# A new instruction order for the first third of a scan-and-FFN kernel, with four small edits

## The chip, the core and the metric

The kernel runs on one core of a Trainium2 chip. A core has five engines with a queue each, which the texts call by short names: PE (TensorE, matrix products; PEld is its loading of the stationary operand), DVE (VectorE), ACT (ScalarE), POOL (GpSimd) and SP (SyncE, which here only issues transfers). Each engine takes its own instructions strictly in the order in which the program gave them, and waits on semaphores for the others. Transfers (DMAs) issued by SP and ACT run on sixteen DMA engines beside all of this. Operands lie in SBUF; products are written to PSUM, which has eight banks of 128 x 512 float32 here.

The metric is the device time of one execution in microseconds (us).

## The reference

One sequence of 2048 tokens with 512 features in bfloat16 goes through a layer norm; the normed tokens go two ways, through a diagonal complex recurrence and through a gated feed-forward net, and the two are multiplied and added to the input:

```python
xn = _layernorm(x)                                   # 2048 x 512
# A: recurrence with 512 complex states
dt = exp(log_dt); Lam_bar = exp(dt * Lam)            # Lam = Lambda_re + i Lambda_im
Bu = xn @ (((Lam_bar - 1) / Lam)[:, None] * Bmat).T
h[t] = Lam_bar * h[t - 1] + Bu[t]                    # over all 2048 tokens
s = 2 * real(h @ Cmat.T) + xn * Dskip
# B: gated FFN, 1376 hidden features
f = (gelu(xn @ w_gate) * (xn @ w_up)) @ w_down
out = x + s * silu(f)
```

## The kernel before

**Tiling.** The tokens are cut into four slabs of 512, and each slab into four tiles of 128 tokens (M = 4). A slab is normed into `xna` (tokens on partitions), turned by one transposing DMA into `xnT` (features on partitions, `dma_t4`), and then used three times:

- `half(s, h)`: the input of the recurrence, two halves of the states a slab. A half is four groups of four products (L528, stationary `BT`, moving `xnT`), each group filling a PSUM bank, which ACT copies to `U` (L530). DVE then turns `U` by the angle tables `tab` into `W` (L540, L548, L552), runs four scans (L559) and turns back into `hst`. That makes the complex recurrence a real one.
- `gate_tile(s, m)`: up and gate products of a tile (L433), evacuated by ACT as copy and gelu (L436) into `ub` and `gt`, multiplied on DVE into `at`; `at_t` transposes `at` by DMA into `atT`; `down_pair` multiplies with the down weights `wd` (L465, eleven products a tile), and ACT evacuates silu into `g2`.
- `skip(s, m)`: `xn * Dskip` on DVE.

`y_tile` then has ACT seed a bank with the skip, PE add `hst @ C2` (L481, eight products), and DVE multiply with `g2` and add x (L486, L491) into an output buffer `ot`, which SP stores. The very last tile is done in two halves of 256 columns (`HD`).

**Slab 0** goes another way, since nothing may wait at the start. Its tiles are only centered (`center`), transposed on PE (`head_t`) and multiplied with the up weights at once (`up_rows`, L382, row block by row block as weights land, and `first_w`, L401); the scale 1/std is applied when ACT evacuates (`out_up`, L391). The up weights come in four row blocks, so that products start with the first. `scale0` makes the normed tokens for `dma_t4(0)` later.

**Tile 0 of slab 0** is on everybody's way. Its mean is made by two engines at once, ACT from the last 128 columns and DVE from the first 384 (L338, L340), then one DVE instruction subtracts both parts (L342) and PE transposes it in two pairs (L312). Before that, PE runs seven products on constants (`dummies`, L295), and between tile 0's and tile 1's transposes one more (`fill`, L301). `parameters` transposes the recurrence's raw parameters `pv` (L584, L585), from which DVE and POOL make the decay `rho`, the step `dt` and the angles.

**The order.** All of this is written as 672 numbered steps. A step is a closure that emits one or a few instructions of one engine (or one DMA), with the steps that it depends on. The functions only record steps; a fixed tuple, found beforehand, says in which order they are emitted, and so each engine's and each DMA queue's order:

```python
for i in ORDER:
    emit, deps = self.steps[i]
    assert deps <= done
    emit()
```

PSUM is shared out as six `ring` banks in turn (`bank()`) and two `ybank`; a group of products can start when the ACT or DVE step that read its bank last is done. A DMA of SP or ACT uses one of eight semaphores in turn, so it is also held until the DMA eight before it has landed.

The lines that the change touches are `ORDER` (L21), `dummies` (L292), `fill` (L298), `center` (L333), `y_part` (L472), and the place where `fill` is called (L644).

Of the kernel before, what the change touches and what calls it, by code (L numbers as in the profile page):

```python
# [11 lines left out]
ALU = mybir.AluOpType  # L12
# [6 lines left out]


ORDER = (  # L21
# [23 lines left out]
)  # L45


# [33 lines left out]
def kernel(  # L81
# [17 lines left out]
    nc = tc.nc  # L99
    P = 128  # L100
# [8 lines left out]
    NS = S // TS  # L109
# [51 lines left out]
    tF = sb("tF", [P, 2, D], FP32)  # L161
    junks = [sb(f"junk{i}", [P, D]) for i in range(2)]
    junk_n = [0]

    def junk():
        junk_n[0] += 1
# [17 lines left out]
    def pe(n, cols, emit, reads=(), writes=(), **kw):  # L184
        return pl.add(PE, n * (cols + 6) / 2400.0, emit, reads, writes, lag=0.22, **kw)
# [106 lines left out]
    def dummies(k, i):  # L292
        def f():
            for j in range(k):
                T.matmul(ybank[j][:] if j < 2 else ring[i][:], lhsT=warm[:, 0:P], rhs=warm, start=True, stop=True)  # L295
        pl.add(PE, k * 0.427, f, [], [("bank", i), ("y", 0), ("y", 1)], lag=0.22, not_before=0.6)

    def fill(k, i):  # L298
        def f():
            for _ in range(k):  # L300
                T.matmul(ring[i][:], lhsT=warm[:, 0:P], rhs=warm, start=True, stop=True)  # L301
        pe(k, 512, f, [], [("bank", i)])

    def head_t(m):

# [27 lines left out]
    def center(m):  # L333

        x = x_tok[:, m, :]
        if m == 0:
            c = 3 * P
            acts(D - c, lambda: act(out=junk()[:, 0 : D - c], in_=x[:, c:D], func=AF.Copy, scale=1.0 / D, accum_out=mb[:, 0:1]),  # L338
                 [("x", 0, 0)], ["mb"], ptr=1, rank=400.0)
            dve(c, lambda: V.tensor_scalar(out=yg[0][:, 0:c], in0=x[:, 0:c], scalar1=1.0 / D, scalar2=None, op0=ALU.mult, op1=ALU.add,  # L340
                                           accum_out=ma[:, 0:1]), [("x", 0, 0)], [("yg", 0, 0), ("ma", 0)], base=0.15, rank=400.0, after=early)
            head.append(dve(512, lambda: V.tensor_scalar(out=xn[0], in0=x, scalar1=ma[:, 0:1], scalar2=mb[:, 0:1], op0=ALU.subtract, op1=ALU.subtract),  # L342
                            [("x", 0, 0), ("ma", 0), "mb"], [("xc", 0, 0), ("xc", 0, 1)], rate=2.3, rank=400.0, after=head[-1:]))
            return
        nmean, key = ma[:, m : m + 1], ("ma", m)
        sums0.append(acts(512, lambda: act(out=junk()[:], in_=x, func=AF.Copy, scale=-1.0 / D, accum_out=nmean), [("x", 0, m)], [key], ptr=2, rank=400.0 - 20 * m))
        dve(512, lambda: V.tensor_scalar(out=xn[m], in0=x, scalar1=nmean, scalar2=None, op0=ALU.add),
            [("x", 0, m), key], [("xc", m, 0), ("xc", m, 1)], rate=2.3, rank=330.0 - 20 * m)
# [123 lines left out]
    def y_part(s, m, c0, c1, bank, key, seed, e):  # L472

        w = c1 - c0
        ps = bank[:, 0:w]
        if seed:
            acts(w, lambda: act(out=ps, in_=sk[s % 2][:, m, c0:c1], func=AF.Copy), [("sk", s % 2, m)], [key])  # L477

        def f():
            for j in range(2 * NPT):  # L480
                T.matmul(ps, lhsT=hst[s % 2][:, j // NPT, j % NPT, m * P : (m + 1) * P], rhs=C2[:, j // NPT, j % NPT, c0:c1],  # L481
                         start=(j == 0 and not seed), stop=(j == 2 * NPT - 1), skip_group_check=True)
        pe(2 * NPT, w, f, [("hst", s % 2, 0), ("hst", s % 2, 1)] + C2S + ([key] if seed else []), [key])
        gi, b = g2s[s, m]
        if seed:
            dve(w, lambda: V.tensor_tensor(out=yg[e][:, c0:c1], in0=ps, in1=g2[gi][:, b, c0:c1], op=ALU.mult), [key, ("g2", gi, b)], [("yg", e, c0)])  # L486
        else:
            ys = tF[:, 0, c0:c1]
            dve(w, lambda: V.tensor_tensor(out=ys, in0=ps, in1=sk[s % 2][:, m, c0:c1], op=ALU.add), [key, ("sk", s % 2, m)], [("tF",)])
            dve(w, lambda: V.tensor_tensor(out=yg[e][:, c0:c1], in0=ys, in1=g2[gi][:, b, c0:c1], op=ALU.mult), [("tF",), ("g2", gi, b)], [("yg", e, c0)])  # L490
        dve(w, lambda: V.tensor_tensor(out=ot[e][:, c0:c1], in0=yg[e][:, c0:c1], in1=x_tok[:, s * M + m, c0:c1], op=ALU.add),  # L491
            [("yg", e, c0), ("x", s, m)], [("ot", e, c0)], rate=2.0)
        mg = s * TS + m * P
        dma(SP, 0.35, 1.5, lambda: nc.sync.dma_start(out=out_td[mg : mg + P, c0:c1], in_=ot[e][:, c0:c1]), [("ot", e, c0)], [("out", s, m, c0)], svc=(2, 0.4, 0.9))

    def y_tile(s, m):
        i = y_n[0] % 2
# [143 lines left out]
    rstd(0, 1)  # L641
    for m in range(1, M):
        norms = rstd(m, m + 1)
    fill(1, 0)  # L644
    head_t(1)
    up_rows(0, 0)
    up_rows(1, 0)
# [174 lines left out]
```

## Time and profile before

| what | us |
|---|---|
| median of three runs (179.24 to 179.58) | 179.26 |
| the profiled execution, known by its span | 178.6 |
| PE busy | 173.4 |
| DVE busy | 156.4 |
| ACT busy | 125.2 |
| POOL busy | 12.0 |

The span goes from the first to the last instruction of the profiled execution; what lies around it is not in the profile. In rows of a timeline the first number is the start in us from the span's start, the second how long the row lasted (several alike in a row are merged, with their number after the x), and in brackets stands the idle time before it and who ended it. `PE`, `DVE`, `ACT` and `POOL` are work, a `q` behind the name is the engine's sequencer, which for `SPq` is the issue of a DMA, not the transfer. In groups, busy time and the mean of one instruction (ns) follow the bar. A product of 512 columns shows 379 ns in such a group, but products overlap: what counts is the distance of their starts.

By stretches of the span, PE, DVE and ACT were busy so:

| stretch, us | PE | DVE | ACT |
|---|---|---|---|
| 0 to 10 | 9.08 | 5.43 | 5.88 |
| 10 to 20 | 10.00 | 6.96 | 9.65 |
| 20 to 30 | 10.00 | 10.00 | 9.60 |
| 30 to 40 | 9.18 | 9.69 | 8.73 |
| 40 to 50 | 10.00 | 7.78 | 8.68 |
| 50 to 60 | 10.00 | 9.51 | 9.41 |
| 60 to 70 | 10.00 | 8.35 | 9.63 |

### The profile page before, as it was taken

To read this page: it belongs to the slowest core of one execution; us is meant where nothing else is said; L and a number is where in the kernel's file an instruction comes from. 1 tells how busy PE (TensorE), PEld (TensorE's weight loads), DVE (VectorE), ACT (ScalarE), POOL (GpSimd) and SP (SyncE) were. 2 spreads that over 40 slices of the span, in tenths; PEclk is the share of its full clock that TensorE was granted. 3 is DMA by queue.
4 is the path that set the end of the run, shared out by engine and by line. 5 is a ranking of instruction groups with operands and counts; after the bars stand their busy time and mean duration, and the time that the engine had idled before them with its cause. 6 is when DMAs were issued, how large, how long until landed. Compare 5 with 4: busy or idle time off the path is not lost.

```text
span 178.6 us, 2428 instructions
## 1 busy us (share of the span) xinstructions
PE 173.4 (97%) x850; PEld 82.8 (46%) x850; DVE 156.4 (88%) x252; ACT 125.2 (70%) x240; POOL 12.0 (7%) x25
## 2 busy tenths in 40 slices
PE   7999999899999999999999999999999999999992
PEld 2555544344445544444445454444444455444451
DVE  3729999999599995899979999899999999999663
ACT  6679999797998999889578865373148618582340
POOL 2462040000200000000040000000000000000000
PEclk9999999999999999999999999999999999999999
DMA  5999999999000809814000075094000006536111
GB/s 159 338 372 188 176 227 315 150 211 228 2 0 0 196 2 173 110 59 81 0 0 6 6 124 129 25 195 84 0 0 0 0 29 155 69 58 135 53 64 60
DMA packets 47507, 18.66 MB, mean 104 GB/s; under 512 B 40232, under 2 KB 46472, under 8 KB 47496
## 3 DMA queue, kind: packets, MB, share of 16 engines
q1 hardware_dynamic: 47472, 18.52, 48.6%
q8 instruction: 6, 0.10, 0.3%
q14 instruction: 5, 0.04, 0.1%
q10 hardware_dynamic: 24, 0.00, 0.0%
HBM read 6.46 MB, written 2.10 MB: 48 GB/s over the span
## 4 chain that ended last, share of the span: by engine, by line
PE 81%; DVE 7%; DMA 6%; ACT 2%; POOL 0%; issue 0%; DVEq 0%
PE ring L433 31%; PE ring L465 20%; PE ybank L481 15%; PE ring L528 12%; DMA atT<-at 5%; PE ring L382 3%; ACT at L391 2%; DVE st L278 1%; DVE Q L620 1%; DMA x_tok<-in_A_x_dram 1%; DVE at L415 1%; DVE yg L486 1%; DVE tab L620 1%; DVE ot L491 1%; DVE sk L364 1%; ACT junk L351 0%
## 5 line engine op out<-in xcount | busy, mean ns | idle before, releaser
L433 PEld LDWEIGHTS <-xnT 128*128 128x128 bf16 x288 | 28.2, 98 | 28.4
L465 PE MATMUL ring<-wd,atT 128*128 128x512 bf16 (+1 forms) x176 | 39.5, 379 | 0.8 <-DMA atT<-at 0.7
L433 PE MATMUL ring<-wg,xnT 128*128 128x512 bf16 (+1 forms) x144 | 31.6, 357 | 0.0
L433 PE MATMUL ring<-wu,xnT 128*128 128x512 bf16 (+1 forms) x144 | 31.3, 357 | 0.0
L528 PE MATMUL ring<-xnT,BT 128*128 128x512 bf16 x128 | 30.1, 379 | 0.0
L559 DVE TENSOR_TENSOR_SCAN Fs<-rho,ini,W 128x512 bf16<-128x512 f32 x24 | 29.7, 1270 | 0.1
L436 ACT ACTIVATE ub<-ring 128x512 bf16<-128x512 f32 (+1 forms) x36 | 19.2, 555 | 14.1 <-PE ring L433 14.0
L481 PE MATMUL ybank<-C,hst 128*128 128x512 bf16 x120 | 27.7, 379 | 0.0
L465 PEld LDWEIGHTS <-atT 128*128 128x128 bf16 (+1 forms) x176 | 17.1, 98 | 22.1 <-DMA atT<-at 1.2
L530 ACT ACTIVATE U<-ring 128x512 bf16<-128x512 f32 x32 | 18.3, 601 | 8.0 <-PE ring L528 8.0
L436 ACT ACTIVATE gt<-ring 128x512 bf16<-128x512 f32 (+1 forms) x36 | 19.5, 555 | 3.7 <-PE ring L433 3.5
L481 PEld LDWEIGHTS <-hst 128*128 128x128 bf16 x136 | 13.3, 98 | 14.0
L528 PEld LDWEIGHTS <-BT 128*128 128x128 bf16 x128 | 12.5, 98 | 14.7
L540 DVE TENSOR_TENSOR Q<-U,tab 128x4096 bf16<-128x4096 bf16 x8 | 18.3, 2291 | 1.0 <-ACT tab L627 0.7
L468 ACT ACTIVATE g<-ring 128x512 f32<-128x512 f32 x16 | 9.3, 595 | 13.6 <-PE ring L465 13.5
L540 DVE TENSOR_TENSOR Q<-Fs,tab 128x4096 bf16<-128x4096 bf16 x8 | 18.3, 2287 | 0.1
L486 DVE TENSOR_TENSOR yg<-ybank,g 128x512 bf16<-128x512 f32 x15 | 10.2, 685 | 5.7 <-PE ybank L481 5.6
L740 ACT ACTIVATE junk<-x_tok 128x512 bf16<-128x512 bf16 x16 | 10.0, 636 | 1.2 <-DMA x_tok<-in_A_x_dram 1.2
L477 ACT ACTIVATE ybank<-sk 128x512 f32<-128x512 bf16 x15 | 9.0, 601 | 1.7 <-DVE yg L486 1.6
L745 ACT ACTIVATE xna<-x_tok,nb,rs 128x512 bf16<-128x512 bf16 x12 | 9.6, 817 | 0.0
L401 PE MATMUL ring<-wg,W 128*128 128x512 bf16 (+1 forms) x48 | 9.5, 357 | 0.0
L559 DVE TENSOR_TENSOR_SCAN Fs<-rho,W 128x512 bf16<-128x512 f32 x8 | 9.3, 1210 | 0.1
(126 smaller groups left out, 171.7 us busy)
## 6 DMA issues: line engine op xcount, KB each, us to landing
out_dram<-ot SPq DMA_DIRECT2D x15, 128.0 KB, 1.7
x_tok<-in_A_x_dram SPq DMA_DIRECT2D x3, 512.0 KB, 9.0
wg<-in_B_w_gate_dram SPq DMA_DIRECT2D x1, 1376.0 KB, 8.1
wd<-in_B_w_down_dram SPq DMA_DIRECT2D x1, 1280.0 KB, 8.7
wu<-in_B_w_up_dram SPq DMA_DIRECT2D x4, 256.0 KB, 3.6
x_tok<-in_A_x_dram SPq DMA_DIRECT2D x4, 128.0 KB, 2.3
wu<-in_B_w_up_dram SPq DMA_DIRECT2D x1, 352.0 KB
atT<-at SPq DMA_TRANSPOSE x16, 3.8
```

The source lines that it names most:

```text
L401: T.matmul(ps[:, 0 : b - a], lhsT=xcT[:, k, m * P : (m + 1) * P], rhs=wt[:, k, a:b], start=(k == 0), stop=(k == KT - 1))
L433: T.matmul(ps[:, 0 : b - a], lhsT=xnT[:, s % 2, m, k, :], rhs=wt[:, k, a:b], start=(k == 0), stop=(k == KT - 1))
L436: acts(b - a, lambda: act(out=dst[:, a:b], in_=ps[:, 0 : b - a], func=AF.Copy if up else AF.Gelu_apprx_tanh), [("bank", r)], [key], table= ...
L465: T.matmul(ps[:], lhsT=atT[:fs, k, m * P : (m + 1) * P], rhs=wd[:fs, k, :], start=(k == 0), stop=(k == NFT - 1))
L481: T.matmul(ps, lhsT=hst[s % 2][:, j // NPT, j % NPT, m * P : (m + 1) * P], rhs=C2[:, j // NPT, j % NPT, c0:c1], start=(j == 0 and not seed ...
L486: dve(w, lambda: V.tensor_tensor(out=yg[e][:, c0:c1], in0=ps, in1=g2[gi][:, b, c0:c1], op=ALU.mult), [key, ("g2", gi, b)], [("yg", e, c0)])
L528: T.matmul(ps[:], lhsT=BT[:, ri, k, pt * P : (pt + 1) * P], rhs=xnT[:, s % 2, :, k, :], start=(k == 0), stop=(k == KT - 1))
L530: acts(512, lambda q=q, ri=ri, ps=ps: act(out=U[ui][:, ri, q, :], in_=ps[:], func=AF.Copy), [("bank", r)], [("U", ui, q, ri)])
L540: dve(4096, lambda: V.tensor_tensor(out=Qf, in0=src.unsqueeze(1).to_broadcast(WQ), in1=table, op=ALU.mult), reads, ["Q"], rate=2.0)
L559: pl.add(DVE, 1.12 if s == 0 else 1.185, lambda ri=ri, q=q, pt=pt, first=first: V.tensor_tensor_scan(out=Fs[:, ri, q, :], data0=rho[:, pt ...
L740: acts(512, lambda i=i, fn=fn, sc=sc, m=m: act(out=junk()[:], in_=x_tok[:, s * M + m, :], func=fn, scale=sc, accum_out=sx[:, s, i, m : m + ...
L745: acts(512, lambda m=m: act(out=xn[m], in_=x_tok[:, s * M + m, :], func=AF.Identity, scale=rs[:, s, m : m + 1], bias=nb[:, s, m : m + 1]), ...
```

## The change

1. `ORDER` is written anew. PE's and ACT's sequences differ up to the gate products of slab 1 and DVE's up to the first y tiles; behind that they are the same. Of SP, the transfers change as below; of POOL, the identity now comes first, the iotas stand behind `dt`, and `ch` and `sh` have moved.
2. `fill` and its call are gone; `dummies` ends with a product of 256 columns more.
3. `center(0)`: ACT's part of the mean is 192 columns instead of 128, DVE's 320 instead of 384. The subtraction is two instructions of 256 columns. In the new order the second half (columns 256 to 511) is emitted first.
4. The last tile's output goes to a third buffer, `junks[0]`, instead of `ot[1]`.

ACT's order at the start was: table load and Silu on a constant (`tiny`), three parameter loads, the means. Now it is: the three parameter loads, a table load, the means of tiles 0 to 2, one eviction, the squares of tile 1, a second table load and Silu, and then the squares of tile 2, the mean of tile 3 and the first Sin.

SP's order, from the gate weights on (the ones before are alike):

| before | after |
|---|---|
| gate weights | gate weights |
| down weights, last 96 rows | slab 1's tokens |
| slab 1's tokens | BT, real part (transposing) |
| Drow | Drow |
| BT, real part (transposing) | xnT of slab 0 |
| xnT of slab 0 | BT, imaginary part |
| BT, imaginary part | down weights, last 96 rows |
| atT of tile 0 | down weights, the other 1280 rows |
| down weights, the other 1280 rows | atT of tile 0 |
| slab 2's tokens | atT of tile 2 |
| atT of tile 2 | atT of tile 1 |
| atT of tile 1 | slab 2's tokens |
| xnT of slab 1 | xnT of slab 1 |
| atT of tile 3 | atT of tile 3 |
| C, real and imaginary | C, real and imaginary |
| slab 1: atT of tile 0 | xnT of slab 2 |
| slab 3's tokens | slab 3's tokens |
| xnT of slab 2 | slab 1: atT of tile 2 |
| slab 1: atT of tile 2, of tile 1 | slab 1: atT of tile 0, of tile 1 |

On ACT, the squares and sums of slab 2's tokens (L740) stand among the evictions of `U` of slab 0's second half in both orders: before, three of them stand ahead of its last three evictions; after, the first stands behind the first silu of slab 0's down products and ahead of one eviction of `U`. On DVE, the coefficients of C (L685 to L703) move from among the `scale0` steps to behind the gate product (`at`) of slab 0's tile 1, and the first two products of the angle tables (L620) move ahead of the last `scale0`.

```diff
 ORDER = (
-    19, 24, 17, 18, 16, 14, 15, 13, 25, 0, 20, 12, 21, 1, 22, 2, 23, 3, 4, 27, 26, 5, 39, 6, 28, 7, 29, 41, ...
+    21, 23, 22, 12, 0, 26, 25, 34, 1, 40, 2, 42, 3, 4, 5, 27, 6, 15, 29, 28, 30, 31, 33, 46, 20, 47, 44, ...
...
     junk_n = [0]
+    ot.append(junks[0])
...
         def f():
             for j in range(k):
                 T.matmul(ybank[j][:] if j < 2 else ring[i][:], lhsT=warm[:, 0:P], rhs=warm, start=True, stop=True)
-        pl.add(PE, k * 0.427, f, [], [("bank", i), ("y", 0), ("y", 1)], lag=0.22, not_before=0.6)
-
-    def fill(k, i):
-        def f():
-            for _ in range(k):
-                T.matmul(ring[i][:], lhsT=warm[:, 0:P], rhs=warm, start=True, stop=True)
-        pe(k, 512, f, [], [("bank", i)])
+            T.matmul(ring[i][:, 0:HD], lhsT=warm[:, 0:P], rhs=warm[:, 0:HD], start=True, stop=True)
+        pl.add(PE, (k + 0.5) * 0.427, f, [], [("bank", i), ("y", 0), ("y", 1)], lag=0.22, not_before=0.6)
...
         if m == 0:
-            c = 3 * P
+            c = 320
...
-            head.append(dve(512, lambda: V.tensor_scalar(out=xn[0], in0=x, scalar1=ma[:, 0:1], scalar2=mb[:, 0:1], op0=ALU.subtract, op1=ALU.subtract),
-                            [("x", 0, 0), ("ma", 0), "mb"], [("xc", 0, 0), ("xc", 0, 1)], rate=2.3, rank=400.0, after=head[-1:]))
+            for i in range(2):
+                h = slice(i * HD, (i + 1) * HD)
+                dve(HD, lambda h=h: V.tensor_scalar(out=xn[0][:, h], in0=x[:, h], scalar1=ma[:, 0:1], scalar2=mb[:, 0:1], op0=ALU.subtract, op1=ALU.subtract),
+                    [("x", 0, 0), ("ma", 0), "mb"], [("xc", 0, i)], rate=2.3)
             return
...
-        dve(w, lambda: V.tensor_tensor(out=ot[e][:, c0:c1], in0=yg[e][:, c0:c1], in1=x_tok[:, s * M + m, c0:c1], op=ALU.add),
-            [("yg", e, c0), ("x", s, m)], [("ot", e, c0)], rate=2.0)
+        o = 2 if (s, m) == (NS - 1, M - 1) else m % 2
+        dve(w, lambda: V.tensor_tensor(out=ot[o][:, c0:c1], in0=yg[e][:, c0:c1], in1=x_tok[:, s * M + m, c0:c1], op=ALU.add),
+            [("yg", e, c0), ("x", s, m)], [("ot", o, c0)], rate=2.0)
...
-        dma(SP, ... out=out_td[mg : mg + P, c0:c1], in_=ot[e][:, c0:c1]) ...
+        dma(SP, ... out=out_td[mg : mg + P, c0:c1], in_=ot[o][:, c0:c1]) ...
...
-    fill(1, 0)
     head_t(1)
```

More of the change, by code (lines that the diff above doesn't have):

```diff
@@ L490, in y_part @@
             dve(w, lambda: V.tensor_tensor(out=yg[e][:, c0:c1], in0=ys, in1=g2[gi][:, b, c0:c1], op=ALU.mult), [("tF",), ("g2", gi, b)], [("yg", e, c0)])
-        dve(w, lambda: V.tensor_tensor(out=ot[e][:, c0:c1], in0=yg[e][:, c0:c1], in1=x_tok[:, s * M + m, c0:c1], op=ALU.add),
-            [("yg", e, c0), ("x", s, m)], [("ot", e, c0)], rate=2.0)
+        o = 2 if (s, m) == (NS - 1, M - 1) else m % 2
+        dve(w, lambda: V.tensor_tensor(out=ot[o][:, c0:c1], in0=yg[e][:, c0:c1], in1=x_tok[:, s * M + m, c0:c1], op=ALU.add),
+            [("yg", e, c0), ("x", s, m)], [("ot", o, c0)], rate=2.0)
         mg = s * TS + m * P
-        dma(SP, 0.35, 1.5, lambda: nc.sync.dma_start(out=out_td[mg : mg + P, c0:c1], in_=ot[e][:, c0:c1]), [("ot", e, c0)], [("out", s, m, c0)], svc=(2, 0.4, 0.9))
+        dma(SP, 0.35, 1.5, lambda: nc.sync.dma_start(out=out_td[mg : mg + P, c0:c1], in_=ot[o][:, c0:c1]), [("ot", o, c0)], [("out", s, m, c0)], svc=(2, 0.4, 0.9))
     def y_tile(s, m):
```

46 rows, old and new, of the table ORDER are left out of this document.

## The prediction

> **What bounds the kernel now.** I read the page's busy line first, then the chain that ended last, then TensorE's own timeline from 0 to 75 us, because the edits end there.
>
> ```profile
> PE 173.4 (97%) x850; PEld 82.8 (46%) x850; DVE 156.4 (88%) x252; ACT 125.2 (70%) x240; POOL 12.0 (7%) x25
> ...
> PE 81%; DVE 7%; DMA 6%; ACT 2%; POOL 0%; issue 0%; DVEq 0%
> ```
> TensorE is the bound: a change pays only where it removes TensorE work or a TensorE wait. Its timeline (start, duration) shows where those are:
>
> ```profile
> 4.06 0.61 PE L312 MATMUL ring<-ident,xna 128*128 128x128 bf16 x4 [0.16 <-DVE xna L342]
> 4.74 0.61 PE L301 MATMUL ring<-const-bfloat16-1.0 128*128 128x512 bf16 x1
> 5.14 0.63 PE L327 MATMUL ybank<-ident,xna 128*128 128x128 bf16 x4
> 5.57 0.75 PE L382 MATMUL ring<-wu,W 128*128 128x512 bf16 x2
> 6.16 0.39 PE L327 MATMUL ybank<-ident,xna 128*128 128x128 bf16 x4
> ...
> 24.76 7.07 PE L528 MATMUL ring<-xnT,BT 128*128 128x512 bf16 x32
> 31.96 2.54 PE L465 MATMUL ring<-wd,atT 128*128 128x512 bf16 x11
> 35.19 4.93 PE L465 MATMUL ring<-wd,atT 128*128 128x512 bf16 x22 [0.69 <-DMA atT<-at]
> 39.95 2.75 PE L528 MATMUL ring<-xnT,BT 128*128 128x512 bf16 x12
> ```
> From 35.19 to 39.95 are 22 products: 0.216 us each. So L528's 32 end at 24.76 + 6.92 = 31.68 and the next starts 0.28 later; its 11 end at 34.34 and the next starts 0.85 later. These **1.13 us** are the only waits I find between 6 and 75 us. The first is the down weights (issued 23.19, 8.7 to landing: 31.9), the second atT of tile 2. The queue shows why:
>
> ```profile
> 21.48 1.66 SPq L449 DMA_TRANSPOSE atT<-at  x1
> 23.19 0.70 SPq L664 DMA_DIRECT2D wd<-in_B_w_down_dram  x1
> 23.93 0.69 SPq L216 DMA_DIRECT2D x_tok<-in_A_x_dram  x1
> 25.86 8.45 SPq L449 DMA_TRANSPOSE atT<-at  x2
> 34.41 2.21 SPq L359 DMA_TRANSPOSE xnT<-xna  x1
> ```
> Two transposes stood behind 1.8 MB of copies. At the head:
>
> ```profile
> 0.72 1.28 ACT L252 ACT_TABLE_LOAD   x1 [0.72 <-PEq L806]
> 2.90 0.31 ACT L338 ACTIVATE junk<-x_tok 128x128 bf16<-128x128 bf16 x1 [0.69 <-DMA x_tok<-in_A_x_dram]
> 3.59 0.41 DVE L342 TENSOR_SCALAR xna<-x_tok,ma,mb 128x512 bf16<-128x512 bf16 x1
> 4.32 0.35 DVE L347 TENSOR_SCALAR xna<-x_tok,ma 128x512 bf16<-128x512 bf16 x1 [0.31 <-ACT junk L346]
> ```
> Until about 5.9 TensorE runs at half rate: four transposes take 0.63 at 5.14 and 0.39 at 6.16.
>
> **The change, part by part.** The new order puts ACT's three parameter loads first, then a table load of its own for the first Copy, and a second one at Silu: ten loads instead of nine. The loads' issues ended at 1.97 before; now the table load runs 1.9 to 3.2, and x (landed 2.88) waits for it. With 64 columns more (0.63 for 512 and 0.31 for 128: 0.05) ACT's part is out at 3.65 instead of 3.31; DVE's, 64 columns shorter, at 3.39. Subtraction starts at 3.68 instead of 3.59. A half costs 0.28 (L491's 256 columns take 0.29, its 512 0.42; 0.41 x 0.29/0.42); two overlap by 0.05 and end at 4.19 instead of 4.00. The new order makes the second half first, while TensorE's first transposes need the first half, so halving hides nothing: transposes start at 4.24 instead of 4.06. The half product more in the warm-up (0.21, to 3.96) and tile 0's parameter transposes (their inputs landed by 3.55) fit before that: free.
>
> Tile 1's transposes wait for L347 (still 4.36 to 4.71, set by ACT's mean of tile 1, landed 3.54), run 4.75 to 5.18, and the first L382 starts at 5.18 instead of 5.57: the filler (0.43) is gone, some of it spent on the later center. That is 0.39 at half rate, **-0.2** once the rate is full. Bounds: -0.4 (all at full rate) and +0.1 (the center 0.3 later still).
>
> [...]
>
> To 24.76 the lead must survive. ACT's second load and Silu (1.48, about 6.1 to 7.6) stand before the squares of tile 2, the mean of tile 3 and Sin; ACT idled 1.62 there (until 8.20). Tile 3's mean is then out at 8.9, its subtraction at 9.5, its transposes due at 10.1. The first eviction starts near 10.4 (10.31 before), first bank reuse is due 0.5 after it. On DVE the seventeen coefficient instructions (13.75 to 15.45) move behind slab 0's tables (first read by tF, 46.98), two table products (1.2 each) move ahead of tile 3's scaling, and DVE's idle 1.77 at 13.75 is filled: xna is complete at 15.3 instead of 16.2. So L528 starts at 24.56. The memsets put among DVE's work (0.06 to 0.07 each) are covered by DVE's wait for tile 0's gelu near 19; iota (0.6, now behind dt on POOL) by the 0.7 that DVE needs for the copy and statistics before it can use it. Without that cover Sin slips by 0.6.
>
> SP: the weights' tail (0.70) and Drow (0.67) no longer precede BT's first transpose, which was issued 7.55 to 15.62: it ends about 0.6 earlier, Drow follows (first read, by skip, near 21), xnT is issued at 15.7 instead of 16.25, BT's second half lands at 23.3 (23.8), due at 25.4. The down weights no longer wait for atT(0) (1.66), so they are issued at 21.6 and, at 8.7, land at 30.3, due 31.5: **-0.28**. atT(0) is now behind them, ready only at 23.9, since DVE does its gate product after statistics and tables. Bounds: it lands at 30.8 (copies done 29.5, one transpose 1.2 as between atT(2), 35.14, and atT(1), 36.31) or 32.4 (1.9 behind the copies, as atT(2) behind slab 2: 33.3 and 35.14). I take 31.7, the latter shortened for the missing slab: wait **+0.2**. atT(2) and atT(1) follow at 32.9 and 34.1, due 34.1 and 36.4: **-0.85**.
>
> Slab 2 (512 KB) moves behind atT(1), issued near 32. Bounds: 3.9 to landing as slab 3 had alone (59.24, 63.1), 9.4 as before: 35.9 to 41.4. With 1.4 MB less ahead of it, it is near the first: 36.5. It now has someone behind it: ACT's first square of slab 2 stands before an eviction of U whose bank slab 1's first L528 needs at about 38.8. Square and eviction take 0.62 + 0.53, so from landing 37.5 on TensorE waits one for one. xnT of slab 1 follows slab 2: 2.5 long (36.3 to 38.83 before), so 38.8 to 39.2 against 38.85; bounds 0 and 0.7, I take **+0.2**.
>
> From 40 to 65, ACT's tF comes earlier (DVE lost 1.95 waiting for it at 48.19), and y of slab 0 one product earlier (L481 at 66.37 before, its hst done 65.8). ACT is 94% busy from 50 to 60; bounds 0 and 0.4 of bank waits, **+0.1**.
>
> The last tile's own buffer: 0. Its L491 rows at 175.05 and 175.71 waited for no store: that of slab 3's tile 1, made by 172.89, had landed (1.7 by the DMA list) at 174.6. The cover is 0.4; a store slower by more would turn the edit into a gain.
>
> Sum: -0.2 - 0.28 - 0.85 + 0.2 + 0.2 + 0.1 = **-0.83**. The profiled execution is known by its span, 178.6; 177.8 then. The runs' median, 179.26, lies 0.66 over the span, so 178.4.
>
> **The rivals.**
> 1. The transposes stay late. Upper ends of atT(0) and xnT plus 0.4: 179.26 - 0.2 - 1.13 + 0.9 + 0.7 + 0.4 = 179.9; with half of these waits 178.9. For: transposes issued behind copies sat in the queue, BT's first for 8.07, the two atT for 8.45. Against: 0.5 MB less stands ahead of them.
> 2. Slower: slab 2's tokens stall ACT, ACT holds U's bank, TensorE waits. From landing 38.5 the whole gain is gone (0.83, and the 0.2 of xnT that the same wait covers); at 39.5 the time is 178.4 + 2.0 - 0.2 = 180.2. For: 9.4 before. Against: less ahead of it.
> 3. TensorE's full rate comes later. Rows bound it: half rate lasted 5.1 us (0.76 to 5.9); if it lasted as long again after the first L382 (5.18), the 4.4 us from 5.9 to 10.3 would be worth half: +2.2, 180.6. [...]
> 4. The new table switch costs more than its row, say two loads (2.56): ACT's mean starts at 4.46, the first L382 near 6.3, all at full rate, 0.6 behind before: 178.4 + 0.8 = 179.2. Against: no ACTIVATE in the trace waits after a load.
>
> [...]
>
> **How the numbers follow.** Forecast 0.50 (own range 177.7 to 178.9), rivals 0.24, 0.15, 0.08, 0.03. 0.2% is 0.36 us, about what runs (179.24 to 179.58) can tell from no change. Faster means under 178.9, slower over 179.6. Rival 1 gives 0.02 faster, 0.16 same, 0.06 slower; rival 2 0.02 same, 0.13 slower; rival 3 slower; rival 4 same: 0.52, 0.21, 0.27. The range, 177.7 to 180.2, leaves out the upper part of rivals 2 and 3 (0.15) and little below.
>
> **What would show it.** Two table loads before 8 us; L312's like at 4.24; first L382 at 5.18; no gap before the second and third down product, a small one before the first; slab 2 landed before 37.5; L528 of slab 1 at 39.0. Wrong if TensorE idles beside ACT's square of slab 2, or if half rate lasts past 6.5.

## The result and the profile after

The changed kernel takes 180.18 us (median of 16 runs, 178.98 to 182.66) against 179.30 (16 runs, 178.60 to 179.99): 1.0058 times the time before, 95% interval 1.0035 to 1.0082. (The ratio leaves out the longest run, of 182.66; the two medians by themselves give 1.0049.) It is slower by 0.6%; I had forecast 178.4.

Yet its profiled execution has a span of 177.4, 1.2 *shorter* than the one of before, and looks as the prediction wanted it. Its page, busy line (16 of its 850 product records are missing) and chain that ended last:

```profile
PE 171.9 (97%) x834; PEld 82.5 (47%) x850; DVE 155.8 (88%) x253; ACT 126.3 (71%) x241; POOL 13.5 (8%) x25
...
PE 94%; DMA 2%; DVE 1%; SPq 1%; issue 1%; DVEq 0%
```

TensorE's timeline of the same execution (start, duration):

```profile
4.39 0.40 PE L308 MATMUL ring<-ident,xna 128*128 128x128 bf16 x4 [0.22 <-DVE xna L340]
4.85 0.40 PE L323 MATMUL ybank<-ident,xna 128*128 128x128 bf16 x4
5.32 0.59 PE L380 MATMUL ring<-wu,W 128*128 128x512 bf16 x2
...
24.60 7.07 PE L527 MATMUL ring<-xnT,BT 128*128 128x512 bf16 x32
31.50 7.30 PE L463 MATMUL ring<-wd,atT 128*128 128x512 bf16 x32
38.64 5.34 PE L527 MATMUL ring<-xnT,BT 128*128 128x512 bf16 x24
```

From 24.60 to 38.64 are 65 products at 0.216 (32 and 33, of which the row shows 32, since one record is missing): neither wait of before is left. The marks of the prediction, for this execution: transposes 4.39 (4.24 forecast), first up product 5.32 (5.18), first half 24.60 (24.56), down weights landed 28.96 (30.3), atT of tile 0 30.98 (31.7), slab 2 35.88 (36.5), slab 1's first half 38.64 (39.0), span 177.4 (177.8).

So two profiles say faster and the runs say slower. The reason is which executions were profiled. Of every run of the experiments, and of the changed kernel's 16, both the time and the span are known, and the time was 1.73 to 1.86 over the span in every one, for every kernel here. The profile of before, 178.6, is thus an execution of about 180.4, longer than all 16 of its runs. Of 148 executions of the kernel before that were measured beside the experiments below, the median span is 177.5, and six reach 178.6. Of 28 executions of the changed kernel (16 and the 12 of e1) the median span is 178.8, and two are at 177.4 or less. I compared an execution from the long end of before's with one from the short end of after's.

### The profile page after: what moved, and what is told of

Read it like the earlier page. It is cut to its first block, busy times and chain, and to the rows that moved or that the text cites. A ratio compares the mean times of both kernels' runs of the same rounds, so it can differ in the third digit from the quotient of the medians.

```text
span 177.4 us, 2421 instructions
## 1 busy us (share of the span) xinstructions
PE 171.9 (97%) x834; PEld 82.5 (47%) x850; DVE 155.8 (88%) x253; ACT 126.3 (71%) x241; POOL 13.5 (8%) x25
## 4 chain that ended last, share of the span: by engine, by line
PE 94%; DMA 2%; DVE 1%; SPq 1%; issue 1%; DVEq 0%
PE ring L431 31%; PE ring L463 21%; PE ring L527 16%; PE ybank L479 14%; PE ring L399 7%; PE ring L380 3%; DMA wu<-in_B_w_up_dram 2%; PE ybank L380 1%; DVE yg L484 1%; SPq L222 1%; DVE junk L490 0%; PE ybank L323 0%; DVE ot L490 0%; DVEq L484 0%
## 5 line engine op out<-in xcount | busy, mean ns | idle before, releaser
L431 PEld LDWEIGHTS <-xnT 128*128 128x128 bf16 x288 | 28.1, 98 | 28.3
L463 PE MATMUL ring<-wd,atT 128*128 128x512 bf16 (+1 forms) x170 | 38.7, 379 | 0.3
L431 PE MATMUL ring<-wu,xnT 128*128 128x512 bf16 (+1 forms) x142 | 31.5, 356 | 0.2
L431 PE MATMUL ring<-wg,xnT 128*128 128x512 bf16 (+1 forms) x142 | 31.2, 356 | 0.1
L527 PE MATMUL ring<-xnT,BT 128*128 128x512 bf16 x128 | 29.6, 379 | 0.0
L479 PE MATMUL ybank<-C,hst 128*128 128x512 bf16 x116 | 27.5, 379 | 0.2
L463 PEld LDWEIGHTS <-atT 128*128 128x128 bf16 (+1 forms) x176 | 17.2, 98 | 20.8
L479 PEld LDWEIGHTS <-hst 128*128 128x128 bf16 x136 | 13.3, 98 | 14.0
L527 PEld LDWEIGHTS <-BT 128*128 128x128 bf16 x128 | 12.5, 98 | 15.0
```

The lines of the kernel that those rows point to most:

```text
L431: T.matmul(ps[:, 0 : b - a], lhsT=xnT[:, s % 2, m, k, :], rhs=wt[:, k, a:b], start=(k == 0), stop=(k == KT - 1))
L463: T.matmul(ps[:], lhsT=atT[:fs, k, m * P : (m + 1) * P], rhs=wd[:fs, k, :], start=(k == 0), stop=(k == NFT - 1))
L527: T.matmul(ps[:], lhsT=BT[:, ri, k, pt * P : (pt + 1) * P], rhs=xnT[:, s % 2, :, k, :], start=(k == 0), stop=(k == KT - 1))
```

## The experiments

In all of them ratio means the time against the kernel before on the same chip, with its 95% interval; 0.1% is 0.18 us. A wait of TensorE is counted from start to start, less 0.216 for each product of 512 columns; the bracket of a row, which goes by modelled ends, shows some 0.16 less. Each trace is of one of a kernel's six to twelve runs; those of e4, e8, e12 and e18 are of the shortest, those of e6 and e17 of the longest. Edits of SP's order are shown as lists of transfers. In e1 to e4 the lines are numbered 2 to 5 lower than in the kernel that each is made from, because the tuple stands in fewer lines.

**e1: the changed kernel again.** The texts of e1 to e4 weigh two theories. By theory 1, the clock, TensorE's step to full rate comes later in some executions of the changed kernel than in others; this is rival 3, a supposition, as no run had shown what sets the step. By theory 2, transfers, TensorE waits for a landing.

> The changed kernel as it is, for its scatter on this chip beside the others of this group and for a second trace. The profiled execution of the changed kernel had a span of 177.4 and none of the waits that I had found before, yet its 16 runs lie from 178.98 to 182.66 around 180.18, and those of the kernel before from 178.6 to 179.99. [...] Theory 2 (transfers): the step is where it was and TensorE waits for a landing between 24 and 75 us. Both: scatter again over 2 us, median 1.003 to 1.008 of before.

1.0072 (1.0045 to 1.0098). This trace (span 179.0, time 180.73) is a usual one, and it shows a wait. TensorE (L523 is L527 of the changed kernel, L459 its L463):

```profile
24.21 7.07 PE L523 MATMUL ring<-xnT,BT 128*128 128x512 bf16 x32
32.66 7.31 PE L459 MATMUL ring<-wd,atT 128*128 128x512 bf16 x33 [1.38 <-DMA atT<-at]
39.80 5.34 PE L523 MATMUL ring<-xnT,BT 128*128 128x512 bf16 x24
```

and SP's issues of the same execution:

```profile
20.86 0.69 SPq L659 DMA_DIRECT2D wd<-in_B_w_down_dram  x1
21.60 0.43 SPq L658 DMA_DIRECT2D wd<-in_B_w_down_dram  x1
23.36 9.90 SPq L443 DMA_TRANSPOSE atT<-at  x3
33.32 0.57 SPq L213 DMA_DIRECT2D x_tok<-in_A_x_dram  x1
```

The 32 products from 24.21 end at 31.11; the next starts at 32.66, 1.5 later. The down weights landed at 29.77 here (28.96 above), atT of tile 0 2.8 behind them (2.0 above), at 32.61. Full rate began at 4.9 by the trace's clock records (four transposes took 0.61 from 4.38 and 0.40 from 4.88), ahead of the first up product at 5.16, so what this execution lost, it did not lose to a late step. So theory 2, transfers; but which one?

**e2 and e3: the filler product.** e2 puts it back into the changed kernel, e3 takes it alone out of the kernel before.

```diff
e2  (head_t, after the second pair of transposes of tile 0)
+                    if i == 1:
+                        T.matmul(ring[0][:], lhsT=warm[:, 0:P], rhs=warm, start=True, stop=True)
e3  (fill)
-            for _ in range(k):
-                T.matmul(ring[i][:], lhsT=warm[:, 0:P], rhs=warm, start=True, stop=True)
+            return
```

> The changed kernel with the filler product back between tile 0's and tile 1's transposes. It costs up to 0.4 on the way to the first up product. Theory 1 (the clock): scatter falls to that of before (1.4) and the median to 178.6 to 179.2, under the changed kernel's. Theory 2 (transfers): scatter as wide as the changed kernel's, median the same or up to 0.4 higher.

> The kernel before, with only the filler product left out. Theory 1 (the clock): its scatter grows to 3 us and its median rises by 0.5 to 1. Theory 2 (transfers): scatter as before, median 0 to 0.3 lower.

e2 1.0072 (1.0038 to 1.0106), runs 179.65 to 182.4; e3 0.9999 (0.9975 to 1.0023), runs 178.80 to 180.22. The filler makes no difference that these runs can tell in either kernel (0.2 to 0.35% either way), and theory 1, which asked for 0.3% and more, falls. (Its rise of 0.5 to 1 us and its scatter of 3 us for e3 were my estimate, which no run shows; the runs show 0.9999 and a scatter of 1.4.) e3's trace, of before's SP order, also shows that the wait for atT of tile 2, 0.85 in the profile of before, isn't a fixed quantity; here it is 0.68:

```profile
34.74 4.93 PE L460 MATMUL ring<-wd,atT 128*128 128x512 bf16 x22 [0.51 <-DMA atT<-at]
```

**e4: only SP's new order, in the kernel before.**

> The kernel before, with only the order of SP's transfers taken from the changed kernel; TensorE, ACT, DVE and POOL keep their orders. Theory 1 (the clock): scatter as before and the median 0 to 1.1 lower (the waits for the down weights and atT of tile 2 go). Theory 2 (transfers): scatter as wide as the changed kernel's, median 0.5 to 1 higher.

1.0133 (1.0102 to 1.0164): SP's order alone is worse than the whole change. TensorE's waits in its trace:

```profile
39.84 1.89 PE L524 MATMUL ring<-xnT,BT 128*128 128x512 bf16 x8 [1.39 <-ACT U L526]
42.23 1.02 PE L524 MATMUL ring<-xnT,BT 128*128 128x512 bf16 x4 [0.51 <-ACT g L464]
...
77.72 2.53 PE L524 MATMUL ring<-xnT,BT 128*128 128x512 bf16 x11 [0.54 <-ACT gt L432]
```

This is the mechanism of rival 2, in a kernel whose ACT does three squares of slab 2 ahead of the last evictions of U: ACT was idle for 4.3 until slab 2 landed at 35.85. The changed kernel's own ACT order avoids that; the wait at 77 was to come back.

**e5, e6, e7, e8: atT of tile 0, and SP as a whole.**

```diff
e5  SP of the changed kernel, and on DVE at(0) last third behind its first part
     BT, imaginary part
+    atT of tile 0
     down weights, last 96 rows
     down weights, 1280 rows
-    atT of tile 0
     atT of tile 2
e6  SP of the kernel before
-    atT of tile 0
     down weights, 1280 rows
+    atT of tile 0
     slab 2's tokens
e7  as e5, and
-    down weights, last 96 rows
     down weights, 1280 rows
+    down weights, last 96 rows
e8  changed kernel, DVE as in e5, all of SP as in the kernel before
```

> The changed kernel with one thing of the new order undone: atT of tile 0 is transferred ahead of both transfers of the down weights, as before the change. For that DVE makes the last third of tile 0's product right behind its first part, some 3 us sooner. In e1 (the changed kernel again) TensorE lost 1.5 at 30.9, waiting for atT of tile 0, which landed 2.8 behind the down weights. Theory A (atT of tile 0 behind the down weights is the loss): the median falls by 0.8 to 1.5 against the changed kernel's, to 178.9 to 179.6 on a chip where before gives 179.3; scatter falls to 1.5 to 2. Theory B (the transfers up to there are late as a whole in most executions, whichever comes last): the down weights come later by the transposition (1 to 1.5) and TensorE waits for them as long: median within 0.3 of the changed kernel's. Theory C (the loss is behind 35 us, slab 2's tokens): no change.

> The kernel before with only this: on SP, atT of tile 0 goes behind the 1280 rows of down weights instead of ahead of them. Theory A: TensorE now waits near 31.7 for atT of tile 0 by 0.5 to 1.5, the median is 0.4 to 1.2 over before's. Theory B and C: within 0.3 of before.

> As e5 (the changed kernel with atT of tile 0 ahead of the down weights), and the last 96 rows of the down weights behind the 1280 (they are the last of a tile's eleven products), so that the 1280 are issued 0.6 sooner. Theory A: a further 0 to 0.5 below e5, the median 0.2 to 0.8 under before's. Theory B: as the changed kernel.

> The changed kernel with SP's whole order taken from the kernel before, and tile 0's product on DVE early as in e5: what is left of the change are the orders of TensorE, ACT, DVE and POOL, the halved center, the missing filler product and the last store's buffer. Theory A and B: the loss was SP's order, so the median is back at before's or up to 0.4 below it, scatter as before's. Theory C, or a loss that the head brings: it stays 0.5 to 1 above before's.

| run | ratio | interval |
|---|---|---|
| e5, atT of tile 0 first | 1.0021 | 0.9994 to 1.0049 |
| e6, before with it last | 1.0016 | 0.9990 to 1.0042 |
| e7, e5 and the tail last | 1.0008 | 0.9979 to 1.0037 |
| e8, all of SP as before | 1.0008 | 0.9980 to 1.0036 |

e8: the loss was SP's order. e5: by the ratios, 0.4 to 0.5% of it, 0.7 to 0.9 us, was the place of atT of tile 0. (e5's interval just meets those of the changed kernel; five kernels against five, below, are clear of each other.) e5 and e8 also have the DVE step earlier that this place needs, and no run of the changed kernel has one without the other. But e4 and e6, with DVE as before, issue the transposition at 22.6, the kernels with the changed DVE order at 23.2 to 24.1, and in all of them it lands 1.8 to 2.8 behind the down weights (1.9 and 2.0 in e4 and e6). So it is the place on SP that counts, as far as these traces tell. e6 is a miss for theory A as I had sized it (0.4 us and up; 0.3 measured, interval up to 0.75), although its trace has the wait: atT of tile 0 landed 1.01 after the first half was done, and TensorE lost 1.05; that trace is of the longest of e6's twelve runs, 181.28 against a median of 179.51, so it shows more than the usual loss. In the traces where this transposition stands behind the down weights, it landed after the first half's end by (a minus: before it) and cost:

| | after | e1 | e2 | e12 | e13 | e4 | e6 |
|---|---|---|---|---|---|---|---|
| landed, us | -0.52 | 1.50 | 0.32 | -0.31 | 1.04 | -0.10 | 1.01 |
| wait, us | 0 | 1.54 | 0.35 | 0 | 1.09 | 0 | 1.05 |

It is the one wait that the prediction put at 0.2; it is anything from 0 to 1.5 as the landing falls.

e8, in which all of SP is as before, has no wait in its trace at all: neither the 0.28 nor the 0.85 of before. (Its span, 177.1, is a short one; its run, 178.91, lies 0.7 under e8's median.)

```profile
24.34 7.07 PE L527 MATMUL ring<-xnT,BT 128*128 128x512 bf16 x32
31.25 7.30 PE L463 MATMUL ring<-wd,atT 128*128 128x512 bf16 x33
38.40 5.34 PE L527 MATMUL ring<-xnT,BT 128*128 128x512 bf16 x24
```

**e9 to e12: slab 2's tokens.** e5 and e7 still had waits of 0.1 to 0.6 near 50 to 57 and 75, e8 none.

```diff
e9  as e8, but on SP
     down weights, 1280 rows
-    slab 2's tokens
     atT of tile 2
     atT of tile 1
+    slab 2's tokens
e10 as e7, and e12 as the changed kernel, but on SP
     atT of tile 2
+    slab 2's tokens
     atT of tile 1
-    slab 2's tokens
e11 as e10, and at the head
     DVE:  +first half of center(0)   second half   -first half
     ACT:  +Silu on a constant   parameter loads   means   -Silu on a constant
```

> As e8 (the changed kernel with SP's order of before), but slab 2's tokens go behind atT of tiles 2 and 1, as the change has them. Theory A (the loss is atT of tile 0 behind the down weights, alone): within 0.3 of e8. Theory D (slab 2's late tokens cost a second part: ACT does the squares of slab 2 later and gives banks back late, which TensorE showed as waits of 0.3 to 0.9 near 50 to 57 and 75 in e1, e2, e5 and e7, and not in e8): 0.3 to 0.8 slower than e8, with such waits in its trace.

> As e7 (atT of tile 0 ahead of the down weights, their last rows behind the 1280), with slab 2's tokens between atT of tile 2 and atT of tile 1, so some 2 to 2.5 sooner. Theory A alone: as e7 (ratio near 1.001). Theory D: the bank waits near 50 to 57 go, 0.3 to 0.6 below e7, so 0.1 to 0.4 below before.

> As e10, and at the head DVE makes tile 0's first half first, and ACT's Silu on a constant stands first again (one table load instead of two). The transposes of tile 0 then start near 3.85 instead of 4.38 (before: 4.06), the first up product can come at 4.75 to 5.1 if tile 1's center is not the later one; up to 0.2 below e10, and not to be told apart from it by its runs if tile 1 or the up weights are the later ones.

> The changed kernel with only slab 2's tokens moved: between atT of tile 2 and atT of tile 1 instead of behind both. Theory A alone: as the changed kernel (1.006 to 1.007 of before), with a wait near 31. Theory D: 0.3 to 0.6 below the changed kernel (1.003 to 1.005), the wait near 31 still there and none near 50 to 57. Were the whole loss slab 2, it would come to 1.001 or less.

e9 0.9984 (0.9965 to 1.0003), e10 1.0004 (0.9979 to 1.0029), e11 1.0037 (1.0011 to 1.0063), e12 1.0053 (1.0023 to 1.0083). In e9 slab 2 is late (it landed at 35.54, in e8 at 32.39) and nothing is lost, neither in its trace nor in its runs; and where it landed latest, at 37.5 and 37.6 in e2 and e1, TensorE lost at most 0.04 near 39. So theory D as written (slab 2's squares) falls; e12, within the intervals, is no better than e1. The traces name another transfer of the same queue. ACT in e2, which lost 0.82 between 49 and 57:

```profile
37.52 0.63 ACT L736 ACTIVATE junk<-x_tok 128x512 bf16<-128x512 bf16 x1 [1.16 <-DMA x_tok<-in_A_x_dram]
...
47.94 1.15 ACT L707 ACTIVATE tF<-hst,cim 128x1024 f32<-128x1024 bf16 x1 [1.14 <-DMA hst<-in_A_C_im_dram]
```

and TensorE, which then waits for ACT's evictions:

```profile
54.08 1.89 PE L429 MATMUL ring<-wg,xnT 128*128 128x512 bf16 x8 [0.22 <-ACT U L527]
```

tF's product needs the imaginary part of C, which stands at the end of this stretch of SP's queue. ACT's idle time ahead of it, and what TensorE lost from the first gate product of slab 1 (L431) to the first y product (L479), which are 18.26 apart where it loses nothing, in all seven traces with the changed ACT order where ACT waited for it (in the others it did not, and TensorE lost nothing there):

| | e5 | e1 | e7 | e13 | e14 | e2 | e17 |
|---|---|---|---|---|---|---|---|
| ACT idle for C, us | 0.48 | 0.78 | 0.91 | 1.00 | 1.06 | 1.14 | 1.45 |
| TensorE's waits, us | 0.15 | 0.45 | 0.58 | 0.67 | 0.74 | 0.82 | 1.12 |

That is 0.33 of reserve, then one for one, to 0.01. The table is a correlation over traces; no run changes C alone. Of the nine traces with the changed ACT order in which slab 2's tokens stand behind atT of tile 1, these seven have the wait (after and e9 have not); of the five that issue them one transposition sooner (e10, e11, e12, e16, e18) none has it. So the remedy of theory D shows in the traces, by way of C, but not in the runs: e10 is like e7, and e12 like e1.

e10 and e11 lost nothing there, but 0.60 and 1.12 at 75. TensorE in e11:

```profile
71.53 3.62 PE L527 MATMUL ring<-xnT,BT 128*128 128x512 bf16 x16
76.11 2.10 PE L527 MATMUL ring<-xnT,BT 128*128 128x512 bf16 x9 [0.96 <-ACT gt L434]
```

ACT, in front of that eviction:

```profile
73.88 0.63 ACT L738 ACTIVATE junk<-x_tok 128x512 bf16<-128x512 bf16 x1 [2.52 <-DMA x_tok<-in_A_x_dram]
```

and SP:

```profile
65.10 1.98 SPq L357 DMA_TRANSPOSE xnT<-xna  x1
67.13 0.94 SPq L217 DMA_DIRECT2D x_tok<-in_A_x_dram  x1
68.18 6.09 SPq L447 DMA_TRANSPOSE atT<-at  x2
```

These are **slab 3's** tokens. The change put them behind xnT of slab 2, so they are issued at 67 instead of 59; ACT's first square of slab 3 stands ahead of evictions of U, as in rival 2, one slab later. In these traces one rule holds to 0.01: TensorE's wait is the landing, less the start of slab 2's first half, less 1.20 (e5 1.34: 0.14; e15 1.70: 0.51; e10 1.80: 0.60; e7 1.84: 0.64; e4 1.91: 0.71; e11 2.32: 1.12; at 0.79 to 0.99, in after, e1, e2 and e12, none).

e11's edits of the head brought tile 0's transposes to 4.20 (4.39 in e10), but the first up product to 5.41 (5.21), 0.04 after its weights landed.

**e13 to e16: slab 3's tokens.**

```diff
e13 as the changed kernel, e14 as e5, e16 as e10, but on SP
     C, real and imaginary
+    slab 3's tokens
     xnT of slab 2
-    slab 3's tokens
e15 as the kernel before, but on SP
     slab 1: atT of tile 0
-    slab 3's tokens
     xnT of slab 2
+    slab 3's tokens
```

> The changed kernel with only slab 3's tokens moved: ahead of xnT of slab 2 (issued near 42) instead of behind it (67 to 69). In six traces with SP's new end of this queue, TensorE waited at about 75 exactly as long as slab 3 landed later than 1.20 after the first product of slab 2's half (landing minus start 0.92: no wait; 1.34: 0.14; 1.80: 0.60; 1.84: 0.63; 1.90: 0.70; 2.32: 1.12). Theory A+E (two losses: atT of tile 0 near 31, and slab 3's tokens near 75, of which an execution that lost at 31 loses less at 75): 0 to 0.5 below the changed kernel, so 1.004 to 1.006 of before; the wait near 31 stays, none near 75. Theory A alone: as the changed kernel.

> The changed kernel with both undone: atT of tile 0 ahead of the down weights (as e5) and slab 3's tokens ahead of xnT of slab 2. Theory A+E: no wait near 31 nor near 75; 0.3 to 0.8 below e5 (1.002), so 0.998 to 1.000 of before. Theory A alone: as e5.

> The kernel before with only slab 3's tokens moved behind xnT of slab 2. Theory A+E: they land between 72 and 74.5, TensorE waits at about 75 by landing minus start of slab 2's half minus 1.2, 0 to 1: median 0.2 to 0.7 above before (1.001 to 1.004). Theory A alone: as before.

> As e10 (atT of tile 0 ahead of the down weights, their last rows behind, slab 2's tokens between atT of tiles 2 and 1) with slab 3's tokens ahead of xnT of slab 2. e10's trace lost 0.60 at 75. Theory A+E: 0.4 to 0.8 below e10 (1.0004), so 0.996 to 0.998 of before, scatter narrow. Theory A alone: as e10.

e13 1.0065 (1.0038 to 1.0092), e14 1.0020 (0.9997 to 1.0044), e15 1.0036 (1.0015 to 1.0057), e16 0.9999 (0.9971 to 1.0027). e15 shows the cause by itself: this one transfer costs the kernel before 0.36% (0.15 to 0.57), and its trace has the wait of 0.51 by the same rule:

```profile
76.08 2.10 PE L528 MATMUL ring<-xnT,BT 128*128 128x512 bf16 x9 [0.34 <-ACT gt L436]
```

In the changed kernel its share can't be told: e13 is like e1, e14 like e5 and e16 like e10, each within the intervals, although none of the three traces has the wait any more. Where TensorE has lost time at 31 already, slab 2's half starts later (73.31 in e1, 71.53 in e11) and slab 3 has landed early enough, as e1's 0.99 shows.

**e17 and e18: the head.** e16's trace had none of the three waits, and another one:

```profile
6.18 0.59 PE L380 MATMUL ring<-wu,W 128*128 128x512 bf16 x2 [0.96 <-DMA wu<-in_B_w_up_dram]
```

```diff
e17 as e9, e18 as e16, but on SP
     tokens of tiles 0 and 1
+    up weights, first row block
     tokens of tile 2
-    up weights, first row block
```

> As e9 (the changed kernel with SP's order of before, slab 2's tokens behind atT of tiles 2 and 1), and the first row block of the up weights is issued ahead of tile 2's tokens instead of behind them. In eleven of twelve traces with the changed head the first up product started within 0.16 of the landing of that block, which lay between 4.91 and 6.14; the forecast had it set by tile 1's transposes, at 5.18. If the block is the later one, it now lands about 0.5 sooner and the first up product is at 5.05 to 5.3 in the trace; median 0 to 0.4 below e9's ratio of 0.9984, so 0.996 to 0.998 of before. If tile 2's tokens become the later ones (then 0.4 to 0.5 later), a wait shows behind the second up product and nothing is won.

> As e16 (atT of tile 0 ahead of the down weights, slab 2's tokens between atT of tiles 2 and 1, slab 3's ahead of xnT of slab 2) with the first row block of the up weights ahead of tile 2's tokens, as in e17. If the block is the later one at the head: first up product at 5.05 to 5.3, median 0.2 to 0.6 below e16's 0.9999, none of the three waits (31, 49 to 57, 75). If not: as e16.

(The count in e17's text is too high: in nine of those twelve traces the product started 0.04 to 0.16 behind the landing, in three 0.18 to 0.29.) 1.0057 (1.0033 to 1.0081) and 1.0053 (1.0033 to 1.0074): slower. The first block landed at 4.47 and 4.61, the first up product came at 5.16 and 5.22, and then tile 2's tokens, at 5.10 and 5.13 instead of 3.8 to 4.6, were the later ones, as the second branch of the expectation has it. TensorE in e17:

```profile
5.16 0.60 PE L380 MATMUL ring<-wu,W 128*128 128x512 bf16 x2
6.35 0.40 PE L323 MATMUL ybank<-ident,xna 128*128 128x128 bf16 x4 [0.59 <-DVE xna L345]
```

How much of the loss this is stays open. e17's trace is of the longest of its nine runs (181.26) and also has waits of 0.46 at 32 and 1.12 from 49 to 57; e18's has none of these, and its gate products begin at 15.81, no later than e16's at 15.92.

**All together.** The five kernels with atT of tile 0 behind the down weights in the new order (after, e1, e2, e12, e13) lie at 1.0053 to 1.0072, the five that differ by having it ahead (e5, e7, e10, e14, e16) at 0.9999 to 1.0021. (e11 and e18, which have it ahead and other edits at the head, lie at 1.0037 and 1.0053.) No kernel is faster than before beyond its interval; e9, at 0.9984 (up to 1.0003), is the nearest.

## Why the prediction was wrong

**The base of the sum.** "The profiled execution is known by its span, 178.6", and "The runs' median, 179.26, lies 0.66 over the span". Time is 1.8 over span, so that execution was 1.1 slower than the median, as much as the two waits that I found in it. Of the traces whose SP order up to there is that of before, e3 has 0.68 of such waits, e8 and e15 none. The traces let one reckon it: in all twenty the span is the start of slab 0's first half, plus 152.7 to 152.8, plus TensorE's waits from there to 78. In the median execution of before (span 177.5) start and waits together are then 24.8; the first half began at 24.24 to 25.54 in the five traces with before's center (mean 24.9), so by this estimate about none of it is waits (0.6 with the earliest of these starts), where I had 1.13. In the median execution of the changed kernel (178.8) they are 26.0; its first half began at 24.09 to 25.21 in eleven traces (mean 24.6), so by the same estimate 1.4 of it is waits, where I had 0.5. This is the step that failed most: -0.28 and -0.85 were taken off a median that mostly doesn't hold them, and the waits that the new order brings were put too low. Without the time of the profiled execution itself, I should have held its waits for anything between 0 and 1.13 in the median, not for 1.13.

**atT of tile 0, +0.2.** The mechanism and the landing were right (31.7 taken; 30.98, 32.61, 32.26, 31.24 and 32.03 in five traces, mean 31.8). The term was not: a wait is never less than nothing, so where landings scatter by 0.8 both ways, the mean of the waits is more than the wait at the mean landing (0.4 here). The five waits are 0, 1.54, 0.35, 0 and 1.09, mean 0.6. And the due time moves too: TensorE was ready at 30.99 to 31.94. Undoing it takes back 0.7 to 0.9 us (e5).

**Slab 2, landing 36.5, threshold 37.5, and xnT of slab 1, +0.2.** Landings of 35.88 to 37.62 were in the bounds, but U's bank was not where it hurt, and xnT cost at most 0.14 (e13). "From 40 to 65, +0.1, bounds 0 and 0.4" holds the place and not the cause: I looked at tF coming earlier on ACT, and not at what tF waits for. C stands behind slab 2 and two transposes on SP; its late landing cost 0.15 to 0.82 in e1, e2, e5, e7, e13 and e14.

**Slab 3** has no term at all. It stands in the table of SP's order, behind xnT of slab 2, and the rule that I used for slab 2 (ACT's square ahead of U's evictions, in order) was never tried on it. It costs the kernel before 0.36% (e15); none of the traces of the changed kernel itself (after, e1) has the wait.

**The head, -0.2.** First up product 5.32 and first half at 24.60: within 0.14 of what was worked out, for that execution. But dropping the filler only moves the wait: the first block of the up weights, landing at 4.91 to 6.14 over the traces, is the later one more often than tile 1's transposes. The gate products began at 15.28 on average in eleven traces with the changed head and at 15.58 in five with before's center (e3, without the filler, among them), a gain of 0.3 that lies well inside their spread (14.80 to 16.25). The kernels whose traces have none of the later waits (e8, e9, e16) don't show it clear of noise in their times (1.0008, 0.9984, 0.9999).

**The halving hides nothing** was right: DVE's two halves ended at 4.33 and the transposes started at 4.39, later than before.

**The last tile's buffer, 0:** from slab 2's first half to the end, the traces that lose nothing there take 105.6 to 105.7, with the third buffer and without. It was not tried alone.

**The rivals.** Rival 1, transposes behind copies land late, is what happened at 31, and its upper end (179.9) was near the median; as I had it, it counted the old waits as gone. Rival 2's mechanism is real (e4, and slab 3), not at the place that I gave. Rival 3, the clock: refuted by e2 and e3; full rate began between 3.64 and 6.16 in all twenty traces, with the filler or without, and earlier in the trace of after (3.84) than in that of before (5.88). Rival 4, the table switch:

```profile
1.95 1.28 ACT L334 ACT_TABLE_LOAD   x1 [1.95 <-issue]
3.24 0.36 ACT L334 ACTIVATE junk<-x_tok 128x192 bf16<-128x192 bf16 x1
...
6.42 1.28 ACT L253 ACT_TABLE_LOAD   x1
7.71 0.20 ACT L253 ACTIVATE tiny<-const-float32-1.0 128x1 f32<-128x1 f32 x1
```

In these rows of ACT after the change each load takes 1.28 and the next instruction starts 0.01 behind it: refuted, as the trace of before had shown already, where the load at 17.25 took 1.28 and the next instruction started at 18.55.

The time, 180.18, lies at the very top of the range, on the other side of no change.

What stays open: how the loss of the changed kernel divides between C and slab 3 (each is within the intervals once atT of tile 0 is dealt with), and why the same transfer lands up to 1.6 apart from one execution to the next (atT of tile 0, 30.98 and 32.61).

## What to carry to other kernels

A profile is one execution: add the usual distance of time and span (1.73 to 1.86 here), find its place among the runs, and only then take its waits for the kernel's. A transfer that is moved later on an in-order queue is priced by its reserve (due less landing) against the scatter of landings, here about 0.8 both ways; the new order ended a wait of 0.85 that one execution had, left the next reader a landing that is 0.4 late on average, and lost. And every transfer behind the moved one has to be followed to its reader, to the end of the reordered stretch: the two that I left out, C and slab 3, both cost time in some of these kernels.

## What the runs showed of the hardware

- Transfers in the same place of the same queue land differently in each execution: the first block of the up weights at 4.91 to 6.14 (4.97 in before, 5.28 in after; issued at 2.1 to 2.2 each time; e17 and e18, which issue it at 1.6, left out). C's imaginary part landed 4.8 behind its issue in after (39.60 to 44.44); in the seven traces above, where ACT's tF waited for it, tF started 6.2 to 7.1 behind that issue (e5 40.80 to 46.98, e17 41.34 to 48.41).
- TensorE's step to full rate came at 5.88 in the trace of before, at 3.84 in that of after, and anywhere from 3.64 to 6.16 over the twenty. Rows show it too: in e4 the last three products on constants took 1.42 from 2.42 (1.48 or 1.49 in the others); in e18 the first two up products still took 1.02 from 5.22 (0.59 in after), and the four transposes from 6.38 took 0.40. Full rate lasted 174.08 in the trace of before and in that of after. What sets the step, no run here shows.
